# QK-normalised attention on one core: one more tile for VectorE, planned further ahead, with TensorE held free for its QKs and a higher activity target

## The chip, the cores and the metric

The kernel runs on one core of a Trainium2 chip. The metric is the device time of one execution in microseconds (us).

## The reference

For each of 32 heads, with 2048 positions of 20 channels in bf16: q and k are normalised to length one, the logits are scaled by one factor per head, softmax, times v.

```python
qn = q / (jnp.sqrt((q * q).sum(axis=-1, keepdims=True)) + eps)
kn = k / (jnp.sqrt((k * k).sum(axis=-1, keepdims=True)) + eps)
logits = jnp.einsum('bhqd,bhkd->bhqk', qn, kn) * t[None, :, None, None]
attn = _softmax(logits, axis=-1)
return jnp.einsum('bhqk,bhkd->bhqd', attn, v)
```

## The kernel before

A head has 16 tiles of 128 keys; a tile has four units of 512 queries. TensorE makes the logits of a unit (QK). Their exponentials are the costly part, and two engines share them. ScalarE takes most units, three at a time (a "wave": `p_ring<-psA`). VectorE takes 3 or 4 tiles of each head: it evicts each unit to a 16-bit integer (`xt<-psD`), makes three integer variants of the tile (`ee`, `ss`, `mm`) and one product (`tt`). TensorE multiplies ScalarE's exponentials and VectorE's `ee`, `ss` and `tt` with v (PV) into one accumulator, `psO`; after the last PV of a head VectorE transposes, divides and stages the output. VectorE also prepares later heads (squares, sums, an inverse square root in small steps, normalised q and k).

The evictions of VectorE go through one bank of PSUM (`psD`, 128x512 in f32), which a QK fills and an eviction reads. So each eviction waits for its QK, and each QK waits for the eviction before it:

```python
t1_prev = [None]
# ... in add_dgroup, for each tile j of head h:
due = h + (j - d0[h] + 0.3) / DVE_TILES[h] - 0.25
for g in reversed(range(NG)):
    qk = add("PE", f"qkD{j}.{g}", lambda ...: qk_mm(e, h, r, g, psD[:, :], tk.rows), PE_MM,
             qk_deps([(h, rg[g], g)]) + [t1_prev[0]] + ..., due - 20000.0)
    qk.rows, qk.work = 0, 0                    # 64 or 128 rows: the planner chooses
    ...
    t1_prev[0] = add("DVE", f"t1.{j}.{g}", lambda ...: e.tensor_scalar(
        xt[sx][:, o:o + 512], psD[:, :], X_MUL, X_ADD, ALU.mult, ALU.add), 0.60,
        [qk] + old("x", NX), due - 5)
# ... then ee, ss, mm, tt of the tile, and three PVs that read ee, ss, tt
```

The order of the instructions on each engine is fixed when the kernel is built, by a list scheduler with assumed durations: an engine that is free takes the ready task with the lowest priority number. It never keeps an engine idle for a task that is about to be ready:

```python
for e in touched:
    if free[e] > now + 1e-9 or not ready[e]:
        continue
    if e == "PE":
        x = min(ready[e], key=lambda r: (r[0] + (0.0 if r[2].name[:2] == last_pe[0] else self.SWITCH), r[1]))
    ...
    else:
        _, _, t = heapq.heappop(ready[e])
```

A second loop repeats the plan. Where the planned TensorE work of a stretch of 3.41 us ("tick") is below `LOAD` columns (a matmul of 512 columns that uses 64 of the 128 rows counts as 256), it lets single QKs there use all 128 rows of the array instead of 64, the other rows being multiplied by zeros. The result is the same; in the plan's count such a QK is worth 512 columns instead of 256.

```python
TICK = 3.41
LOAD = 3072.0
...
while i and load < self.LOAD and m >= i:
    if pe[m].work == 0 and pe[m].rows == 64 and pe[m] not in more:
        more.add(pe[m])
        work[m] += 256.0
        load += 256.0
    m -= 1
```

## Time and profile before

| | before |
|---|---|
| timed, us | 739.66 median of 3 (738.92 to 740.25) |
| profiled execution, us | 744.0, span 742.3, mean granted clock 0.983 |
| ScalarE busy, us | 730.0 |
| VectorE busy, us | 724.2 |
| VectorE's last product ends, us | 735.9 |
| ScalarE's last exponential ends, us | 738.1 |

In the pages PE is TensorE, PEld its weight loads, DVE VectorE, ACT ScalarE and POOL GpSimd. First, the page's busy times (us, share of the span, instructions) and the granted clock in 40 slices (tenths):

```profile
PE 638.9 (86%) x4974; PEld 163.2 (22%) x4996; DVE 724.2 (98%) x1334; ACT 730.0 (98%) x546; POOL 3.2 (0%) x20
...
PEclk8799999999999999999999999999999999999999
```

ScalarE and VectorE are both full. Which of them ends last is a matter of a few us, so their waits decide. The waits of ScalarE and then of VectorE (us in total, times, longest):

```profile
ACT p_ring L585 <- PE psA L506: 5.0, 8, 1.1
```

```profile
DVE xt L618 <- PE psD L506: 9.2, 14, 2.0
DVE oT L533 <- PE psO L521: 2.8, 1, 2.8
```

VectorE loses 9.2 us in 14 waits for the QK of its own units. The 2.8 us are the wait for the very last PV: VectorE had nothing left to do. The windows view gives busy time in stretches, with the granted clock (PEclk) after the five engines:

```profile
131.00:134.00 3.00, 1.69 (x13) 0.33 (x9) 3.00 (x5) 3.00 (x3) 0.00 (x0) 0.93 0.44 73
134.00:137.00 3.00, 2.67 (x14) 0.73 (x13) 2.15 (x4) 2.51 (x3) 0.00 (x0) 0.50 0.71 42
...
714.00:717.00 3.00, 1.97 (x12) 0.42 (x11) 3.00 (x5) 3.00 (x4) 0.00 (x0) 1.00 0.00 0
717.00:720.00 3.00, 2.65 (x11) 0.58 (x12) 1.71 (x4) 2.65 (x2) 0.00 (x0) 0.54 0.00 0
```

In each pair TensorE does less for a while, then gets half its clock, and in that stretch both VectorE (third busy time) and ScalarE (fourth) lose time. In the clock records of this trace the granted clock is either 1.00 or 0.50. It is 0.50 in one stretch of 13.65 us (14.10 to 27.75 us), in three of 3.41 us each (from 133.56, 672.87 and 717.24 us), and from 741.13 us to the end. That more work for TensorE keeps it up was the assumption, from these pairs of stretches.

### The profile page before, as it was taken

Reading aid. Unit: us, or ns where it says so; the run is one execution under the profiler, and the core shown is the slowest. Engines: PE = TensorE matmul, PEld = TensorE weight load, DVE = VectorE, ACT = ScalarE, POOL = GpSimd, SP = SyncE. Lnnn points to the kernel's source line nnn. Section 1 sums busy time; section 2 is a strip of 40 time slices with the busy share of each in tenths; the row PEclk is TensorE's granted clock in tenths of the full one; section 3 lists DMA queues with packets and bytes.
Section 4 is the critical chain, followed back from the end, with each engine's and each line's share of the span. In section 5 each row is a group of like instructions: output and inputs, shape, how many; then the busy total and the mean of one; then the engine's idle time right before and its main releaser. Section 6 shows DMA issues by size and latency. Waiting matters only on the chain.

```text
span 742.3 us, 12574 instructions
## 1 busy us (share of the span) xinstructions
PE 638.9 (86%) x4974; PEld 163.2 (22%) x4996; DVE 724.2 (98%) x1334; ACT 730.0 (98%) x546; POOL 3.2 (0%) x20
## 2 busy tenths in 40 slices
PE   8987888888898888898888888888889888888896
PEld 2122222222222222222222222222222222222221
DVE  8899999999999999999999999999999999999986
ACT  7899999999999999999999999999999999999997
POOL 1000000000000000000000000000000000000000
PEclk8799999999999999999999999999999999999999
DMA  5333233232233233223233323323323323330100
GB/s 62 77 41 57 50 64 46 29 61 52 52 50 48 44 61 57 55 39 52 42 61 61 50 34 54 61 46 56 55 45 46 58 44 56 58 56 19 34 1 10
DMA packets 196650, 36.10 MB, mean 49 GB/s; under 512 B 172528, under 2 KB 196592, under 8 KB 196592
## 3 DMA queue, kind: packets, MB, share of 16 engines
q1 hardware_dynamic: 196448, 35.22, 29.9%
q8 instruction: 39, 0.64, 0.4%
q14 instruction: 19, 0.16, 0.1%
q10 hardware_dynamic: 144, 0.08, 0.0%
HBM read 7.87 MB, written 2.62 MB: 14 GB/s over the span
## 4 chain that ended last, share of the span: by engine, by line
ACT 94%; PE 3%; DVE 1%; POOL 0%; SPq 0%; DMA 0%; issue 0%; ACTq 0%; POOLq 0%
ACT p_ring L585 94%; PE psA L506 1%; PE psO L521 1%; PE psD L506 1%; SPq L290 0%; DMA qk_sb<-in_q_dram 0%; DVE sq L389 0%; DVE qz L480 0%; POOL vaug L293 0%; POOL qkn L293 0%; DVE rs_sum L391 0%; DVE oT L533 0%; DVE xt L618 0%; ACTq L255 0%; DVE o_stage L543 0%
## 5 line engine op out<-in xcount | busy, mean ns | idle before, releaser
L585 ACT ACTIVATE p_ring<-psA 128x1536 bf16<-128x1536 f32 x538 | 723.1, 1731 | 5.3 <-PE psA L506 5.0
L506 PE MATMUL psA<-qz,kR 64*128 64x512 bf16 (+1 forms) x1200 | 291.2, 390 | 61.2 <-ACT p_ring L585 56.1
L618 DVE TENSOR_SCALAR xt<-psD 128x512 int16<-128x512 f32 x436 | 296.7, 680 | 10.6 <-PE psD L506 9.2
L521 PE MATMUL psO<-p_ring,vaug 128*32 128x512 bf16 x1612 | 156.7, 390 | 1.1 <-ACT p_ring L585 0.9
L506 PE MATMUL psA<-qz,qkT 64*128 64x512 bf16 x398 | 128.8, 386 | 20.5 <-ACT p_ring L585 18.7
L506 PE MATMUL psD<-qz,kR 64*128 64x512 bf16 x318 | 124.1, 390 | 10.8 <-DVE xt L618 8.3
L632 DVE TENSOR_TENSOR tt<-xt,mm 128x2048 f16<-128x2048 f16 x109 | 132.2, 1213 | 0.2
L506 PEld LDWEIGHTS psA<-qz,kR 64*128 64x128 bf16 x1210 | 63.0, 94 | 200.7 <-ACT p_ring L585 186.4
L626 DVE TENSOR_SCALAR ee<-xt 128x2048 int16<-128x2048 int16 x109 | 74.4, 683 | 0.2
L630 DVE TENSOR_SCALAR mm<-xt 128x2048 int16<-128x2048 int16 x109 | 74.4, 683 | 0.0
L628 DVE TENSOR_SCALAR ss<-xt 128x2048 int16<-128x2048 int16 x109 | 74.4, 682 | 0.0
L521 PEld LDWEIGHTS psO<-p_ring,vaug 128*32 128x32 bf16 x1612 | 40.1, 94 | 103.3 <-issue 99.3
L506 PEld LDWEIGHTS psD<-qz,kR 64*128 64x128 bf16 (+1 forms) x326 | 30.5, 93 | 81.2 <-DVE xt L618 57.1
L506 PEld LDWEIGHTS psA<-qz,qkT 64*128 64x128 bf16 (+1 forms) x402 | 31.7, 94 | 65.2 <-ACT p_ring L585 58.5
L506 PE MATMUL psD<-qz,qkT 64*128 64x512 bf16 (+1 forms) x110 | 42.5, 386 | 3.2 <-DVE xt L618 2.4
L521 PE MATMUL psO<-tt,vaug 128*32 128x512 f16 x436 | 43.9, 393 | 1.2 <-ACT p_ring L585 0.7
L521 PE MATMUL psO<-ss,vaug 128*32 128x512 f16 x436 | 43.8, 391 | 0.0
L521 PE MATMUL psO<-ee,vaug 128*32 128x512 f16 x436 | 43.6, 390 | 0.0
L389 DVE TENSOR_TENSOR sq<-qk_sb 128x640 f32<-128x640 bf16 x32 | 26.1, 814 | 0.2 <-DMA qk_sb<-in_q_dram 0.2
L391 DVE TENSOR_REDUCE rs_sum<-sq 128x32 f32<-128x640 f32 x32 | 25.7, 804 | 0.1
L533 DVE STREAM_TRANSPOSE oT<-psO 128x512 f32<-128x512 f32 x32 | 22.6, 706 | 2.8 <-PE psO L521 2.8
L417 DVE TENSOR_TENSOR qkn<-qk_sb,rs_r 128x640 bf16<-128x640 bf16 x31 | 25.2, 814 | 0.0
(43 smaller groups left out, 138.7 us busy)
## 6 DMA issues: line engine op xcount, KB each, us to landing
kR<-qkT SPq DMA_DIRECT2D x62, 96.0 KB, 2.1
qz<-qkT SPq DMA_DIRECT2D x124, 32.0 KB, 1.9
kR<-qkT SPq DMA_DIRECT2D x62, 64.0 KB, 2.0
qk_sb<-in_k_dram SPq DMA_DIRECT2D x32, 80.0 KB, 2.1
vaug<-in_v_dram SPq DMA_DIRECT2D x32, 80.0 KB, 3.3
qk_sb<-in_q_dram SPq DMA_DIRECT2D x124, 20.0 KB, 2.5
out_dram<-o_stage SPq DMA_DIRECT2D x31, 80.0 KB, 1.6
kR<-qkT SPq DMA_DIRECT2D x62, 32.0 KB, 1.9
```

What stands on the lines that cost most here:

```text
L389: s1 = dv("sq", lambda e, tk, x=x: e.tensor_tensor(sq[:, :, :], x[:, :, :], x[:, :, :], ALU.mult), 0.735, lds[h] + last_sum + (q0[2:] if h ...
L391: sums.append(dv("sum", lambda e, tk, i=i: e.tensor_reduce(rs["sum"][:, 2 * R * i:2 * R * (i + 1)], sq[:, :, :], AXIS_X, ALU.add), 0.73, [ ...
L417: norm[h] = dv("norm", lambda e, tk, x=x, b=b, i=i: e.tensor_tensor(qkn[b][:, :, 0:D], x[:, :, :], bc(rs["r"][:, 2 * R * i:2 * R * (i + 1) ...
L506: return eng.matmul(dst, lhsT, mov, tile_position=(p0, 0))
L521: last = eng.matmul(psO[32 * g:32 * g + 32, :], vaug[h % NV][:, r_of(g), :], rhs_of(g), start=start, stop=False, skip_group_check=True, ti ...
L533: trO[h] = add("DVE", f"tr{h}", lambda e, tk: e.transpose(oT[:, :, :].rearrange("p r d -> p (r d)"), psO[:, :]), 0.63, [lambda: pv_users[h ...
L585: act[w] = add("ACT", f"exp{w}", lambda e, tk: e.activation(p_ring[:, p0 * 512:p0 * 512 + n], psA[:, slot * WAVE * 512:slot * WAVE * 512 + ...
L618: t1_prev[0] = add("DVE", f"t1.{j}.{g}", lambda e, tk, o=o: e.tensor_scalar(xt[sx][:, o:o + 512], psD[:, :], X_MUL, X_ADD, ALU.mult, ALU.a ...
L626: te = dv("e", lambda e, tk: e.tensor_scalar(ee[se][:, 0:w], x, 0x7C00, KE_BITS, ALU.bitwise_and, ALU.bitwise_or), 0.533, t1s + old("e", NE))
L628: t5 = dv("s", lambda e, tk: e.tensor_scalar(ss[se][:, 0:w], x, float(SHIFT - 4096), None, ALU.add), 0.533, t1s + old("s", NE))
L630: tm = dv("m", lambda e, tk: e.tensor_scalar(mm[sm][:, 0:w], x, 0x3FF, 0x3800, ALU.bitwise_and, ALU.bitwise_or), 0.533, t1s + old("m", NM))
L632: tT = dv("T", lambda e, tk: e.tensor_tensor(tt[se][:, 0:w], x.bitcast(FP16), mm[sm][:, 0:w].bitcast(FP16), ALU.mult), 1.067, [tm] + old(" ...
```

## The change

Intent: one tile more goes from ScalarE to VectorE (109 become 110). VectorE's tiles are planned 0.8 of a head ahead instead of 0.25, and the preparation further ahead too (`LEAD`, `SPREAD`). In the plan, TensorE may stay idle for up to 0.1 us when a QK for VectorE is about to be ready and another task would delay it ("hold"). The hold of 0.0 for VectorE's evictions never holds anything, as the code shows. The activity target rises from 3072 to 3500 columns.

```diff
@@ class Program
-    LOAD = 3072.0
+    LOAD = 3500.0
...
+    HOLD = {"DVE": 0.0, "PE": 0.1}
@@ list_schedule
+        soon = {"DVE": {}, "PE": {}}
+
         def arrive(t, when):
             heapq.heappush(events, (when, 0, t.seq, t))
+            if t.name[:2] == "t1" or t.name[1:3] in ("kD", "2D"):
+                soon[t.eng][t.seq] = when
+
+        def hold(e, now, dur):
+
+            return any(now < w <= now + self.HOLD[e] and now + dur > w + 0.03 for w in soon[e].values())
...
+                held = []
+                if e in soon:
+                    held = [r for r in ready[e] if r[2].name[:2] not in ("t1", "tr") and hold(e, now, r[2].dur)]
+                    if len(held) == len(ready[e]):
+                        continue
+                    if held:
+                        ready[e] = [r for r in ready[e] if r not in held]
+                        heapq.heapify(ready[e])
... (soon[] is emptied as tasks become ready; held tasks go back to the queue)
@@ kernel
-    LEAD = 2.4
-    SPREAD = 0.6
+    LEAD = 3.0
+    SPREAD = 1.0
     PE_MM = 0.23
-    DVE_TILES = [4 if h % 8 in (1, 4, 6) or h == 31 else 3 for h in range(H)]
+    DVE_TILES = [4 if h % 8 in (1, 4, 6) or h in (8, 31) else 3 for h in range(H)]
...
-                due = h + (j - d0[h] + 0.3) / DVE_TILES[h] - 0.25
+                due = h + (j - d0[h] + 0.3) / DVE_TILES[h] - 0.8
```

More of the change, by code (lines that the diff above doesn't have):

```diff
@@ L130, in list_schedule @@
                     heapq.heappush(ready[t.eng], (t.pri, t.seq, t))
+                    if t.eng in soon:
+                        soon[t.eng].pop(t.seq, None)
             for e in touched:
@@ L140, in list_schedule @@
                     _, _, t = heapq.heappop(ready[e])
+                for r in held:
+                    heapq.heappush(ready[e], r)
                 t.start = now
```

## The prediction

> **What bounds it now.** ScalarE. The chain of waits that ended last is 94% ScalarE exponentials; they run without a gap in stretches of 106, 536 and 40 us, at 536.09/399 = 1.344 us for one wave of three 512-column units (groups of instructions: 537 full waves and one wave of a single unit, 741 ns). From the first exponential (10.4 us) to the end of the last (738.1 us), ScalarE waits only 5.0 us (waits of ScalarE): 2.5 us before 27 us, then 0.5, 0.5, 1.1 and 0.4 us near 27, 136, 676 and 720 us. The windows view shows a granted clock of 0.5 before each: a start at half clock from 14 to 28 us, and single dips near 134-137, 673-677 and 717-721 us. VectorE is nearly as full: 724.2 of 742.3 us busy, practically 25.0 in each 25 us from 50 to 650 us. Its 18 us of idle: about 6 us are start, last wait and output (0.9 + 2.8 + 2.1); about 9 us are waits for the QK of its own tiles (2.8 us before 27, 3.0 in 27-50, 3.3 in 700-722, 1.1 after). Its last tile is done at 735.9, 2.3 us before ScalarE.
>
> **What the change does.**
> - One tile (four units) moves from ScalarE to VectorE: 1612 units become 1608, 538 waves become 536 full ones. ScalarE loses one full wave and the single one: about 1.8 us, all on the critical path.
> - VectorE gains four evictions, three integer steps and a product: 7 x 0.60 + 1.13 = 5.4 us (starts in the timeline), busy 724 to about 729.5 us.
> - The 0.8-head lead and the TensorE hold (at most 0.1 us of TensorE idle) reorder work so that VectorE's QK is there in time. The relative order against the preparation hardly changes, as both move by about 0.55-0.6 head. They must pay for the 5.4 us out of the 9 us of QK waits.
> - 3500 columns: more single QKs with 128 rows instead of 64 (only 42 now). A 128-row QK costs the same time alone[...]; TensorE has 103 us idle. The aim is to avoid the half-clock dips. [...] Without them ScalarE regains up to 2 us; the start probably stays slow.
>
> **Sum.** Floor from ScalarE: 742.3 - 1.8 - 5.0 = 735.5 us of profiled span; floor from VectorE: 729.5 + 6 = 735.5. The two are now balanced, so each remaining stall of either counts. I expect about 3-5 us of them: some 739.7 of span, that is 2.5 us less, so 737.2 us timed (739.66 before). Range 734.2 to 740.4. Within 2%: 0.98.
>
> **What would show it.** 536 exponential waves, ScalarE busy about 728 us; 440 evictions, VectorE about 729.5 us; VectorE's waits for QK down from 9 to about 4-5 us; more 128-row matmuls (over 100); fewer half-clock windows after 30 us (3 to 0 or 1); the dips' ScalarE waits gone; VectorE's last product at or after the last exponential, so that the chain's end may pass through VectorE.
>
> **What would make it wrong.** VectorE becomes the bound: if its waits don't shrink, the added 5.4 us ends behind ScalarE and the time rises 1-2 us. The ring of three tile buffers, freed only by PV of the same head, may block a 0.8-head lead (2.7 tiles). Delayed preparation might starve ScalarE. Or the clock recovers at the start too, and the gain is 4-5 us. Spread between runs (1.3 us) is comparable with the effect.

The sum: 742.3 - 1.8 - 5.0 = 735.5 us for ScalarE, 735.5 for VectorE, and 3 to 5 us of stalls make the 739.7 us of span and 737.2 us timed. The "up to 2 us" that ScalarE regains are an estimate from its waits of 0.5, 1.1 and 0.4 us at the three single dips.

## More of the kernel before

In the trace of before, two QKs that follow each other start within 0.03 us 580 times, and both have 64 rows each time; where one of the two has 128 rows, the starts are at least 0.22 us apart. The median recorded duration of a QK is 0.39 us for both.

The profiled execution was 4.3 us slower than the median of the timed ones.

## The result

The changed kernel took 737.33 us (median of 4, 736.92 to 737.65); in the same rounds the kernel before took 739.61 (738.92 to 740.25). The ratio is 0.9969, 95% interval 0.9952 to 0.9986. A ratio is the mean time of one kernel's runs over that of the other's of the same rounds, so not quite the ratio of the medians. It is 2.3 us faster, clear of noise.

The lines that answer to those of before. The page:

```profile
PE 645.1 (88%) x4953; PEld 172.1 (23%) x5004; DVE 726.2 (99%) x1342; ACT 727.3 (99%) x544; POOL 3.2 (0%) x20
...
PEclk9999999999999999999999999999999999999999
```

The waits, of ScalarE and of VectorE:

```profile
ACT p_ring L606 <- PE psA L527: 0.8, 1, 0.8
```

```profile
DVE oT L554 <- PE psO L542: 3.3, 1, 3.3
DVE xt L639 <- PE psD L527: 1.0, 2, 0.8
```

The same windows:

```profile
131.00:134.00 3.00, 2.08 (x17) 0.69 (x20) 3.00 (x7) 3.00 (x3) 0.00 (x0) 1.00 0.45 64
134.00:137.00 3.00, 3.00 (x28) 0.63 (x20) 3.00 (x6) 3.00 (x4) 0.00 (x0) 1.00 0.75 68
...
714.00:717.00 3.00, 2.93 (x28) 0.78 (x31) 3.00 (x5) 3.00 (x3) 0.00 (x0) 1.00 0.00 0
717.00:720.00 3.00, 2.93 (x32) 0.65 (x24) 2.88 (x6) 3.00 (x3) 0.00 (x0) 1.00 0.09 27
```

The end of the chain of waits:

```profile
698.82 30.90 ACT p_ring L606 x23
729.72 1.35 ACTq L276
731.07 0.04 issue
731.12 0.43 PE psO L542 x4
```

ScalarE waits for data only at its first wave (0.8 us). VectorE's waits for QK fell from 9.2 to 1.0 us although it does more, and its last product (728.2 us) ends 2.8 us before the last exponential (731.1 us). But a good part of the 9.2 us belongs to the profiled execution of before: 3.8 us of it fall before 50 us, around the half clock at 14 to 28 us, and in e1 below, without the hold but with no half clock before the end of its trace, these waits are 2.7 us. No half clock is left before the last microsecond of the span. The span of 735.2 us is close to what ScalarE's work alone allows.

But one must not subtract the two spans (742.3 and 735.2). The timed runs say 2.3 us, not 7: the profiled execution of before had 13.7 us of half clock near its start, and most of its executions cannot have had that. Of the 33 in the experiments 24 have a mean granted clock of 0.992 or more, which leaves room for less than 13 us at half clock in all (worked out from the mean and the span).

### The profile page after: what moved, and what is told of

Same layout as the page of the kernel before. It is cut to its first block, busy times and chain, and to the rows that moved or that the text cites. A ratio compares the mean times of both kernels' runs of the same rounds, so it can differ in the third digit from the quotient of the medians.

```text
span 735.2 us, 12564 instructions
## 1 busy us (share of the span) xinstructions
PE 645.1 (88%) x4953; PEld 172.1 (23%) x5004; DVE 726.2 (99%) x1342; ACT 727.3 (99%) x544; POOL 3.2 (0%) x20
## 4 chain that ended last, share of the span: by engine, by line
ACT 97%; DVE 1%; DMA 0%; POOL 0%; SPq 0%; PE 0%; ACTq 0%; issue 0%; POOLq 0%; DVEq 0%
ACT p_ring L606 97%; DMA qk_sb<-in_q_dram 0%; SPq L311 0%; ACTq L276 0%; DVE qz L501 0%; POOL vaug L314 0%; POOL qkn L314 0%; DVE sq L410 0%; DVE rs_sum L412 0%; DVE oT L554 0%; DVE xt L639 0%; PE psA L527 0%; DVE o_stage L564 0%; PE psO L542 0%; PE psD L527 0%
## 5 line engine op out<-in xcount | busy, mean ns | idle before, releaser
L542 PE MATMUL psO<-p_ring,vaug 128*32 128x512 bf16 x1608 | 148.4, 384 | 4.3 <-issue 3.0
L527 PE MATMUL psA<-qz,qkT 64*128 64x512 bf16 (+1 forms) x394 | 126.8, 384 | 16.5 <-ACT p_ring L606 14.0
L527 PE MATMUL psD<-qz,kR 64*128 64x512 bf16 (+1 forms) x317 | 121.9, 385 | 11.3 <-DVE xt L639 8.0
L527 PEld LDWEIGHTS psA<-qz,kR 64*128 64x128 bf16 (+1 forms) x1207 | 69.5, 93 | 194.8 <-ACT p_ring L606 160.3
L542 PEld LDWEIGHTS psO<-p_ring,vaug 128*32 128x32 bf16 x1608 | 38.5, 94 | 71.7 <-issue 67.3
L527 PE MATMUL psD<-qz,qkT 64*128 64x512 bf16 (+1 forms) x102 | 39.3, 386 | 4.3 <-DVE xt L639 3.5
```

Of the source, the lines that this page charges most:

```text
L527: return eng.matmul(dst, lhsT, mov, tile_position=(p0, 0))
L542: last = eng.matmul(psO[32 * g:32 * g + 32, :], vaug[h % NV][:, r_of(g), :], rhs_of(g), start=start, stop=False, skip_group_check=True, ti ...
```

## The experiments

Theories at the start: **W**, the gain is the ScalarE work that was taken away; **C**, the gain is the clock, by the columns, and the tile pays only on top of it. After the first set came **P** (the lead and spread make room on VectorE) and **H** (the hold does). Every kernel below computed the right result and ran six times; the kernel before ran 11 times in each set of four. Each set ran on another chip. "Last product" and "last exponential" are the ends of the last such instruction in the trace; where the product is later, VectorE ends last. Each trace is of one execution: those of e8 and e9 were at a clock of 0.991 and 0.995, with single stretches of half clock, and that of e6 has one such stretch near 12 us; the others have none before the last 8 us.

| kernel | time us, median (range) | granted clock, lowest to highest | ratio to before, 95% | last product / last exponential, us |
|---|---|---|---|---|
| set 1: before | 740.07 (738.82 to 743.82) | 0.983 to 0.997 | | |
| e1 tile only | 739.90 (739.16 to 742.35) | 0.989 to 0.998 | 1.000 (0.998 to 1.002) | 733.3 / 731.8 |
| e2 columns only | 744.83 (744.81 to 745.02) | 0.995 to 0.997 | 1.0062 (1.0045 to 1.0079) | 738.7 / 733.2 |
| e3 all but the tile | 738.65 (738.63 to 738.91) | 0.997 to 0.999 | 0.9979 (0.9960 to 0.9998) | 722.8 / 732.7 |
| e4 all but the columns | 736.93 (736.62 to 738.80) | 0.993 to 1.000 | 0.9959 (0.9940 to 0.9977) | 730.0 / 730.7 |
| set 2: before | 739.88 (738.86 to 745.38) | 0.981 to 0.997 | | |
| e5 the whole change | 737.02 (736.96 to 737.06) | 0.999 to 1.000 | 0.9949 (0.9922 to 0.9976) | 728.3 / 731.1 |
| e6 all but the lead | 736.92 (736.90 to 737.66) | 0.998 to 1.000 | 0.9950 (0.9920 to 0.9980) | 731.0 / 731.7 |
| e7 all but the hold | 742.22 (741.98 to 742.27) | 0.997 to 0.999 | 1.0019 (0.9991 to 1.0046) | 736.1 / 732.7 |
| e8 tile and lead | 742.78 (740.77 to 743.72) | 0.991 to 0.999 | 1.0023 (0.9993 to 1.0052) | 737.8 / 737.0 |
| set 3: before | 739.85 (738.75 to 745.63) | 0.983 to 0.998 | | |
| e9 tile and hold | 738.16 (736.56 to 740.53) | 0.988 to 0.999 | 0.9968 (0.9940 to 0.9996) | 730.6 / 732.5 |
| e10 hold for tiles 95 up only | 738.58 (738.53 to 738.62) | 0.998 to 1.000 | 0.9974 (0.9947 to 1.0002) | 732.1 / 732.7 |
| e11 hold for tiles 0 to 94 only | 737.39 (737.35 to 738.30) | 0.996 to 1.000 | 0.9960 (0.9935 to 0.9985) | 731.3 / 731.4 |
| e12 111 tiles | 740.10 (739.91 to 740.45) | 0.997 to 0.998 | 0.9995 (0.9970 to 1.0020) | 734.1 / 731.6 |

### Set 1: tile and columns, each alone and each taken away

e1, the tile alone:

```diff
-    DVE_TILES = [4 if h % 8 in (1, 4, 6) or h == 31 else 3 for h in range(H)]
+    DVE_TILES = [4 if h % 8 in (1, 4, 6) or h in (8, 31) else 3 for h in range(H)]
```

> The kernel before with 110 tiles, nothing else of the change. Theory W (the gain is ScalarE work: 1.8 us less of exponentials): about 1.8 us faster than before, 737.8. Theory C (the gain is clock: half-clock windows no longer stall ScalarE and VectorE, and the tile only pays on top of it): no gain, 739 to 742, because VectorE has 5.4 us more to do and still loses about 9 us waiting for QK; its last product then comes after the last exponential.

Measured: no gain. The end of its chain of waits shows why; it goes through VectorE:

```profile
730.84 0.60 DVE ss L628
731.44 0.61 DVE mm L630
732.05 0.02 issue
732.08 1.24 DVE tt L632
733.32 0.04 issue
733.36 0.43 PE psO L521 x4
```

VectorE's waits for QK in this trace:

```profile
DVE xt L618 <- PE psD L506: 2.7, 7, 0.5
```

ScalarE was done early and VectorE was not: W fails. C's number held, and so did its VectorE that ends last; the 9 us of waits that it counted on did not (2.7 us here). That the clock is not the gain, the next run shows.

e2, the columns alone:

```diff
-    LOAD = 3072.0
+    LOAD = 3500.0
```

> The kernel before with 3500 columns asked, nothing else. Theory C: half-clock windows between 30 and 720 us go from 3 to 0 or 1, the start runs at full clock as in the changed kernel, ScalarE's waits fall under 2 us, and the time falls by 1 to 2 us (737.5 to 738.6) with mean clock at or over 0.995. Theory W: no change within 0.5 us (739.2 to 740).

Measured: 744.83 us, 4.8 us slower than before; a miss for both theories. The clock did what C said: full from the start to 736 us, and ScalarE waited 0.8 us. Still the kernel is slower, because VectorE's last product now ends at 738.7 us, 5.6 us after the last exponential. The clock alone is not the gain. VectorE's waits for QK:

```profile
DVE xt L618 <- PE psD L506: 5.0, 10, 0.8
```

e3, the changed kernel with 109 tiles:

```diff
-    DVE_TILES = [4 if h % 8 in (1, 4, 6) or h in (8, 31) else 3 for h in range(H)]
+    DVE_TILES = [4 if h % 8 in (1, 4, 6) or h == 31 else 3 for h in range(H)]
```

> The changed kernel with 109 tiles. Theory W: 1.8 us slower than the changed kernel (739.1), as 537.3 waves instead of 536 sit on ScalarE, which never waits. Theory C: within 0.7 us of the changed kernel (737.3 to 738.0), the clock staying at 0.996 or more.

Measured: 738.65 us, 1.6 us slower than the control e5 (737.02, from another set; the two medians of before differ by 0.2). So with the rest of the change the tile pays nearly its whole 1.8 us of ScalarE. VectorE's waits:

```profile
DVE oT L554 <- PE psO L542: 10.4, 1, 10.4
```

Without the tile VectorE stands idle for 10.4 us at the end: the rest of the change has made room there. The tile fills part of it and moves the last product from 722.8 to 728.3 us, by 5.5 us (costed at 5.4).

e4, the changed kernel with 3072 columns:

```diff
-    LOAD = 3500.0
+    LOAD = 3072.0
```

> The changed kernel with 3072 columns asked. Theory C: half-clock windows come back (clock 0.98 to 0.992), and 1 to 2.5 us are lost (738.3 to 740). Theory W: at most 0.5 us lost.

Measured: 736.93 us, nothing lost in the median. Five of its six runs had a clock of 0.998 or more and one had 0.993 and took 738.80. C falls: the room on VectorE does not come from the columns.

### Set 2: lead and hold

e5 is the changed kernel again, as the control.

> The changed kernel itself, as the control of this set: 737.0 to 737.6, mean clock 0.996 to 0.999, no ScalarE wait after the first wave.

Measured: 737.02 us, six runs within 0.1 us. ScalarE waited once more after the first wave, 0.4 us near 13 us, so not quite as expected.

e6, the changed kernel with the lead and spread of before:

```diff
-    LEAD = 3.0
-    SPREAD = 1.0
+    LEAD = 2.4
+    SPREAD = 0.6
-                due = h + (j - d0[h] + 0.3) / DVE_TILES[h] - 0.8
+                due = h + (j - d0[h] + 0.3) / DVE_TILES[h] - 0.25
```

> The changed kernel with LEAD, SPREAD and the 0.25-head lead of before (tile, hold and 3500 columns stay). Theory P (the plan of VectorE's work, that is lead and spread, makes the room for the tile): VectorE's last product lands after the last exponential, 739 to 744, as in the tile alone (739.9) or the columns alone (744.8). Theory H (the hold of TensorE makes the room): within 0.5 us of the control.

Measured: 736.92 us, the same as the control. P falls.

e7, the changed kernel without the hold:

```diff
-    HOLD = {"DVE": 0.0, "PE": 0.1}
+    HOLD = {"DVE": 0.0, "PE": 0.0}
```

> The changed kernel with a hold of 0 for TensorE (tile, lead and 3500 columns stay). Theory P: within 0.5 us of the control. Theory H: VectorE waits over 3 us more for QK, ends last, and the time is 738.5 to 741.

Measured: 742.22 us, 5.2 us slower than the control, more than H expected. VectorE's waits:

```profile
DVE xt L639 <- PE psD L527: 5.7, 10, 0.9
```

They are 4.7 us more than in the changed kernel, and the last product ends 7.8 us later; the rest is 0.6 us of other idle time and 2.5 us of busy time (727.2 against 724.7 us in the control, up to the last product). The timeline of e7 shows one of the ten waits (start us, duration us, engine, line, operation, tiles, and in brackets the idle time before):

```profile
702.89 0.68 DVE L639 TENSOR_SCALAR xt<-psD 128x512 int16<-128x512 f32 x1
...
703.72 0.40 PE L542 MATMUL psO<-p_ring,vaug 128*32 128x512 bf16 x4
...
704.05 0.39 PE L527 MATMUL psD<-qz,kR 64*128 64x512 bf16 x1
...
704.48 0.69 DVE L639 TENSOR_SCALAR xt<-psD 128x512 int16<-128x512 f32 x1 [0.90 <-PE psD L527]
```

The eviction ends at 703.57 us and frees the bank. At 703.72 TensorE starts four PVs, so the QK starts only at 704.05, 0.33 us later, and with nothing else planned VectorE is idle for 0.90 us. The bank had been free for 0.15 us when the PVs began, and still the QK started behind them. Whether TensorE could have taken it first was not shown; what the change alters is the plan, and there the QK goes first. The control at about the same time, one tile further on, reads:

```profile
700.61 0.68 DVE L639 TENSOR_SCALAR xt<-psD 128x512 int16<-128x512 f32 x1
...
701.21 0.48 DVE L564 TENSOR_TENSOR o_stage<-oT,rec 128x320 bf16<-128x320 f32 x1
701.35 0.09 PEld L527 LDWEIGHTS psD<-qz,kR 64*128 64x128 bf16 x1 [0.44 <-DVE xt L639]
701.35 0.39 PE L527 MATMUL psD<-qz,kR 64*128 64x512 bf16 x1
701.61 0.68 DVE L647 TENSOR_SCALAR ee<-xt 128x2048 int16<-128x2048 int16 x1
702.21 0.68 DVE L639 TENSOR_SCALAR xt<-psD 128x512 int16<-128x512 f32 x1
```

The weight load stands 0.44 us idle for the eviction and the QK starts 0.06 us after the eviction's end at 701.29 us. The next eviction follows without idle time, after two other operations. The two evictions of e7 above stand in the control at 695.76 and 697.57 us, with `ee` and `ss` between them and no idle time.

e8, the kernel before with the tile and the lead, without hold and columns (the edits are those of e1 and the reverse of e6's).

> The kernel before with the tile, LEAD, SPREAD and the 0.8-head lead; no hold, 3072 columns. Theory P: as fast as the changed kernel, 736.6 to 737.6. Theory H: 739 to 740.5, like the tile alone.

Measured: 742.78 us. P fails again. Even its best run (740.77 at a clock of 0.999) is 3.8 us over the control.

### Set 3: the hold alone, early and late, and one tile more

e9, the kernel before with the tile and the hold alone (the changed kernel with the edits of e4 and e6 together).

> The kernel before with the tile and the hold only (lead, spread and 3072 columns of before). Theory H (the hold alone makes the room for the tile): 736.6 to 737.6, VectorE's last product before the last exponential. Rival (the hold needs one of its companions, each of which alone was dispensable): 739 or more.

Measured: between the two expectations, 738.16 us with a wide spread. At a clock of 0.998 and 0.999 it took 736.56 and 736.61 us, as good as the control; at 0.995 to 0.988, 738.0 to 740.5 us. VectorE's last product ends before the last exponential. The best execution of e1, the same version without the hold, took 739.16 us at the same clock of 0.998, in set 1: 2.6 us for the hold alone. The hold alone does make the room; what is missing in this version is a steady clock.

e10 and e11 use the hold for a part of VectorE's tiles:

```diff
# e10
-            if t.name[:2] == "t1" or t.name[1:3] in ("kD", "2D"):
+            if t.name[:2] == "t1" or t.name[1:3] in ("kD", "2D") and int(t.name[3:].split(".")[0]) >= 95:
# e11: the same with < 95
```

> The changed kernel, holding TensorE only for QKs of VectorE's tiles 95 to 109 (the last four heads, where no preparation of a later head is left to fill VectorE's wait). Theory E (the hold matters at the end, where two evictions follow each other with nothing between): 737 to 738.5. Theory S (it matters all along, VectorE falls behind steadily): 739.5 to 742.

> The changed kernel, holding TensorE only for tiles 0 to 94. Theory E: 740.5 to 742.2, QK waits of 0.5 to 0.9 us come back after 690 us. Theory S: 737 to 739.

Measured: 738.58 (late only) and 737.39 (early only), against 742.22 with none and 737.02 with all. Neither E nor S holds alone; e11 met S's number and e10 came nearer to E's. The last product says how: 736.1 us with no hold, 732.1 with the late one (4.0 us earlier), 731.3 with the early one (4.8 us earlier), 728.3 with both (7.8 us earlier). The halves nearly add up on VectorE. The time does not follow all the way, because ScalarE then ends last, at 731.4 us with the early hold and 732.7 us with the late one, where it waited 1.4 us for PVs (1.1 us of it near 251 us, before any hold, as in e7).

e12, 111 tiles:

```diff
-    DVE_TILES = [4 if h % 8 in (1, 4, 6) or h in (8, 31) else 3 for h in range(H)]
+    DVE_TILES = [4 if h % 8 in (1, 4, 6) or h in (8, 16, 31) else 3 for h in range(H)]
```

> The changed kernel with one more tile for VectorE (111, head 16). ScalarE loses 4 units (1.8 us), VectorE gains 5.4 us, of which 2.8 us are free (last product 728.2, last exponential 731.0 in the control) less the 1.8 us by which ScalarE now ends earlier: VectorE becomes last by some 4 us against ScalarE's new end, 738 to 740. If VectorE had hidden room, it would be 735 to 736.

Measured: 740.10 us, just over the upper end expected. The last product moves by 5.8 us to 734.1 us and VectorE ends last. There is no hidden room: of 109, 110 and 111 tiles, 110 is the best for this plan.

### What the thirteen plans say together

Where the hold covers all of VectorE's tiles and there are 110 of them (e4, e5, e6, e9), the last product ends at 728.3 to 731.0 us and before the last exponential. Without the hold and with the same tiles (e1, e7, e8) it ends at 733.3 to 737.8 us and after it. This holds with and without columns and lead, so it is not one lucky order of instructions.

How the hold does it can be counted in the traces. An eviction that follows another with no other VectorE work between costs at least 0.48 us of idle time, even where its QK starts 0.06 us after the first one's end. There are 6 to 9 such pairs in every plan without the hold (before, e1, e2, e7, e8), 0 to 3 in those with it (e3 to e6, e9, e12), and 4 and 5 with half of it (e10, e11). PVs stood before the QK in four of e7's eight pairs and in none of e1's six. So the hold does two things: it lets a QK go before PVs, and it gives a plan in which other work stands between the evictions. The runs do not separate the two.

The columns go with the clock. Of the 52 listed executions with 3500 columns (the first result's 4 and six each of e2, e3, e5 to e7 and e10 to e12), 3 had a clock of 0.995 or less, all three of e2, whose trace (0.995) has half clock in its last 7 us alone. Of the 57 with 3072 columns (33 of before in the three sets, six each of e1, e4, e8, e9), 36 had. Each pair of plans that differ in the columns alone goes the same way (before and e2, 24 of 33 and 3 of 6; e8 and e7, 4 and 0 of 6; e9 and e6, 4 and 0; e4 and e5, 1 and 0). With the hold, the tile and no lead, the columns are worth 1.2 us in the median (e9 738.16, e6 736.92) and nothing at full clock (736.56 and 736.90). With the lead they are worth nothing in the median (e4 736.93, e5 737.02), though e4 still had one slow execution.

No version beat the control clearly: e6 and e4 are within 0.1 us of it.

## Why the prediction was right or wrong

The predicted time was 737.2 us and the measured one 737.33. The sign and the size are right; some terms of the sum were not.

- *The tile takes 1.8 us from ScalarE.* Right. ScalarE has 536 waves and is busy for 727.3 us. The fastest executions of set 2 are 738.86 before and 736.96 after, 1.9 us apart; taking the tile out of the changed kernel costs 1.6 us (e3).
- *VectorE pays 5.4 us.* Right for the place where it ends (5.5 us between e3 and e5). The busy time grew by less (721.6 to 726.2, 4.6 us), and 729.5 was predicted from before's 724.2.
- *Lead and hold together must pay for it.* The step was too coarse. The hold pays (without it 5.2 us are lost), the lead pays nothing measurable (without it -0.1 us).
- *3 to 5 us of stalls remain, VectorE's waits for QK fall to 4-5 us, its last product comes at or after the last exponential.* This is the term that was mis-sized. The waits fell to 1.0 us and VectorE ends 2.8 us before ScalarE; ScalarE keeps one wait of 0.8 us at its start. The profiled span of 735.2 us is the predicted floor of 735.5, not the predicted 739.7.
- *The base of the sum.* 742.3 us was the span of an execution that took 744.0 us. The 33 executions of before had medians of 739.85 to 740.07 us, and the fastest took 738.75. Counting the slow profile as typical and leaving 3 to 5 us of stalls were two errors of opposite sign, and that the time came out so near is luck in these two terms. (The list of the 9 us of waits counts one of 2.0 us in two windows: 3.8 us fall before 50 us, 1.1 between 50 and 690 and 4.4 after.) In set 2 the gain of 2.9 us in the medians is 1.9 us at the best executions and some 1.0 us of spread, which goes with the clock: before's median is 1.0 us over its own best, the control's 0.06.
- *3500 columns: over 100 of the QKs with 128 rows, fewer dips.* Right: in the trace of e5, where no matmul record is missing (5004 matmuls, 5004 weight loads), 327 have 128 rows, against the 42 recorded before, and there is no half clock before the end. "The start probably stays slow" was wrong: the start at half clock was of that execution.

Why the columns alone (e2) delay VectorE so much can be read from its trace, though no run tests it. Against e3, which also has 109 tiles, its last product ends 15.9 us later. It waited 5.0 us for QK (e3: not at all), and its small steps of the inverse square root take 34.7 us, summed from start to next start, against 25.9 (28.1 in before). They stand more often right behind one another, 66 times against 12 (before: 16), and then a start follows the last after 0.225 us in the median, against 0.10 where another operation follows. The two sums overlap a little, where an eviction waits right after a small step, and the rest is not broken down. Open is why this plan puts the small steps so. What is shown is that with the hold the columns cost nothing measurable (e4 against e5, e9 against e6 at full clock).

## What to carry to other kernels

When two engines share a load, moving a piece between them can be worth nothing until the receiver has room (e1), so first find what keeps the receiver waiting; here it was a single-bank round trip through TensorE, and letting TensorE idle for at most 0.1 us in the plan ended the receiver's work 7.8 us earlier. The scheduler of before could not find this, as it never waits for what is about to be ready. And before explaining a change from two profiles, compare the profiled executions with the timed ones: here nearly 5 of the 7 us between the spans came from one unlucky execution.

## What was measured of the clock and of the single bank

- In before, half clock came with TensorE busy for 1.69 of the 3.00 us near its start (131 to 134 us) and 1.97 of 3.00 us (714 to 717 us), and no single gap in the first of them was over 0.8 us (matmuls and weight loads agree in number there, so hardly a record is missing). How much work would have kept the clock full was not shown. Giving more QKs 128 instead of 64 rows, at a TensorE busy share of 88% against 86%, went with 3 of 52 executions at a clock of 0.995 or less, against 36 of 57.
- Half clock was not only near the start: in the trace of before the clock was full up to 14 us, then half for 13.7 us, and half again three times between 130 and 721 us, for 3.41 us each. For a kernel this tight such stretches matter: the same kernel took 738.75 to 745.63 us in set 3, at clocks of 0.996 and 0.983, three times the effect studied.
- With a single bank that TensorE must refill after each eviction, and nothing between two evictions, VectorE was idle for 0.48 us when the QK started at once and 0.77 to 0.90 us when PVs stood before it (e7).
